# Linear attention with routed experts: deeper load buffers, later expert weights, and scatters that skip empty slots and do not order each other

## The chip, the cores and the metric

The kernel runs on one core of a Trainium2 chip. The metric is the device time of one execution in microseconds; the time before is the median of five runs. A core has five engines that run their own queues in order: TensorE (PE in the profile, with PEld for its weight loads), VectorE (DVE), ScalarE (ACT), GpSimd (POOL) and SyncE (SP). DMAs are issued from GpSimd's and SyncE's queues and run on 16 DMA engines.

## The reference

`q`, `k`, `v` are [8, 8, 576, 64] (batch, heads, sequence, head width). Softmax of q is over the head width, softmax of k over the sequence; the attention output has its heads put side by side, so that it is a table of 4608 tokens by 512. Every token belongs to one of eight experts, by `domain_id`, and goes through that expert's two matrices with a ReLU between them.

```
q_s = exp(q - max(q)); q_s = q_s / sum(q_s, over d)
k_s = exp(k - max(k)); k_s = k_s / sum(k_s, over s)
kv  = einsum('bhsd,bhse->bhde', k_s, v)
x   = einsum('bhsd,bhde->bhse', q_s, kv)      # then to [4608, 512]
for e in range(8):
    m = domain_id == e
    out[m] = relu(x[m] @ w1[e]) @ w2[e]       # w1 512x1024, w2 1024x512
```

Inputs and output are float32. The kernel works in float16 with float32 sums.

## The kernel before

It has two parts, and the instructions are put in order by a scheduler that follows what depends on what and how many buffers a pool has; the text of the program gives the priority.

**Attention, per batch (`emit_batch`).** Three DMAs of GpSimd's queue load k, q and v of the batch (96 partitions, each six sequence rows of eight heads) and turn them to float16. `k_raw` and `q_raw` share one tag of the pool `apool`, which has two buffers, so there is one buffer for each; `v_sb` has two. ScalarE makes `ke` and `qe` (exponentials, L323 and L326). VectorE adds the six rows of `ke` in five instructions (L335 to L339, tiles `ks01`, `ks23`, `ks45`). TensorE transposes `qe` in 24 pieces (L346), which ScalarE copies from PSUM to `qT_sb` in three instructions (L353). For each of four pairs of heads TensorE computes k transposed times v (L360, 12 matmuls into `kv_ps`) and the column sums of `ke`, by one matmul of `ks01` with a column of ones (L367, into `tab_ps`); VectorE takes the reciprocal and scales the pair into the block matrix `kvp` (L375 to L382). For each of six rows j, TensorE multiplies `qT_sb` by `kvp` into two tiles, `xpsA` and `xpsB` (L397; the tag has two buffers), and VectorE divides each by its softmax sum into `x_sb` (L408, L410). A DMA of SyncE's queue writes `x_sb` to `attn_x_scratch` (L416).

**Routing.** Each expert has 704 slots, 5632 in all, for 4608 tokens. Early instructions on VectorE give each token its slot and a second slot behind the expert's count, so that most empty slots get a copy of a token. The table from slot to token is made with compares (`emit_mask_chunk`, four chunks, tiles `spm` and `sce`, L254 to L274) and matmuls, and ends in `perms_sb` (L305).

**Experts, per group of 512 slots (11 groups, `emit_gather` and `emit_group`).** Four indirect DMAs of GpSimd's queue gather 128 token rows each (L449); TensorE transposes them (L470), multiplies by w1 (L493), ScalarE applies ReLU (L501), TensorE multiplies by w2 (L512), VectorE copies each 128 rows to `out_stage` (L519), and an indirect DMA of GpSimd's queue scatters them to the output rows (L531). Slots of a second copy write the same values to the same row once more. Since all scatters write the one output tensor, each waits until the scatter before it has landed. `xG` has three buffers.

**Weights.** `load_weights(e)` (L144) issues two DMAs of 1024 KB (as float16) on GpSimd's queue; `wpool` has four buffers. In the text, experts 0 and 1 stand behind the last batch, and expert 2 and later ones in the loop over groups, by this table:

```
late_load = {0: [2], 1: [3], 2: [4], 3: [5], 5: [6], 6: [7]}
```

Loads of experts 0 to 3 wait for no buffer, and the scheduler puts them wherever GpSimd's queue has nothing of higher priority.

## Time and profile before

| | us |
|---|---|
| median of five runs | 378.2 |
| lowest and highest | 377.34, 379.39 |
| the profiled execution | 379.95 |
| its span, first to last instruction | 378.2 |

| engine | busy us | share of the span |
|---|---|---|
| TensorE, matmuls | 257.4 | 68% |
| TensorE, weight loads | 159.1 | 42% |
| VectorE | 151.6 | 40% |
| GpSimd | 120.5 | 32% |
| ScalarE | 113.0 | 30% |

The mean granted clock of TensorE is 0.821 of its full 2.4 GHz. The shares are means over stages that differ: the attention stage ends with the first gather, at 153 us, the expert stage's matmuls run from 164 to 348 us, and behind them the core still writes. So each stage is to be read by itself: which engine is busy in it, and which wait ends last.

### The profile page before, as it was taken

The numbers are of one execution on the slowest core, as the hardware profiler recorded it, in microseconds if no ns is written. First come the engines' busy times: TensorE is split into PE (matmuls) and PEld (weight loads), VectorE is DVE, ScalarE is ACT, GpSimd is POOL, SyncE is SP. The second block draws the span as 40 slices with busy tenths as digits, with TensorE's granted clock in tenths as the row PEclk, the third lists the DMA queues.
The fourth block names the chain that finished last, engine by engine and source line by source line (L and its number), as shares of the span: only waits on it lengthen the run. The fifth ranks groups of instructions, "written<-read, shape, count | busy, mean of one in ns | idle before, by whom it ended". The sixth has DMA issues, their size and how long they took to land.

```text
span 378.2 us, 4999 instructions
## 1 busy us (share of the span) xinstructions
PE 257.4 (68%) x2010; PEld 159.1 (42%) x2010; DVE 151.6 (40%) x488; ACT 113.0 (30%) x129; POOL 120.5 (32%) x143
## 2 busy tenths in 40 slices
PE   0365547545484874279999999999998897988000
PEld 0353426424363552134756445575544455533000
DVE  7986566687374896022240322403223021222000
ACT  2573746270706300022404225042240222231000
POOL 5320302122110000673726244360644353223232
PEclk9999999655555555569999999999999698999655
DMA  6999999999999314232399676269269222122111
GB/s 95 204 209 204 184 216 230 204 236 206 240 205 237 54 51 125 72 99 81 113 180 206 125 135 163 71 149 197 88 125 231 90 98 97 57 83 83 58 75 64
DMA packets 38055, 53.32 MB, mean 141 GB/s; under 512 B 2320, under 2 KB 28944, under 8 KB 38032
## 3 DMA queue, kind: packets, MB, share of 16 engines
q0 software_dynamic: 36992, 48.24, 64.5%
q1 hardware_dynamic: 1040, 4.76, 3.6%
q8 instruction: 16, 0.26, 0.3%
q14 instruction: 7, 0.06, 0.0%
HBM read 67.67 MB, written 16.25 MB: 222 GB/s over the span
## 4 chain that ended last, share of the span: by engine, by line
PE 39%; DMA 33%; issue 17%; ACT 4%; DVE 3%; POOL 3%; POOLq 0%; ACTq 0%; DVEq 0%
PE hT_ps L493 20%; PE out_ps L512 18%; DMA q_raw<-in_q_dram 15%; DMA out_dram<-out_stage,perms_sb 9%; DMA k_raw<-in_k_dram 7%; DMA xG<-attn_x_scratch,perms_sb 2%; POOL xG L449 2%; ACT qe L326 2%; DVE xT L478 1%; ACT ke L323 1%; DVE out_stage L519 1%; ACT qT_sb L353 1%; PE tpsA L470 1%; POOLq L592 0%; POOL out_dram L531 0%
## 5 line engine op out<-in xcount | busy, mean ns | idle before, releaser
L501 ACT ACTIVATE hT_sb<-hT_ps 128x512 f16<-128x512 f32 x88 | 50.6, 596 | 158.2 <-PE hT_ps L493 158.0
L493 PE MATMUL hT_ps<-xT,w_sb 128*128 128x512 f16 (+7 forms) x576 | 84.6, 309 | 4.0 <-DVE xT L478 4.0
L519 DVE COPY out_stage<-out_ps 128x512 f32<-128x512 f32 x44 | 30.4, 692 | 140.2 <-PE out_ps L512 140.2
L512 PE MATMUL out_ps<-w_sb,hT_sb 128*128 128x512 f16 (+1 forms) x384 | 82.0, 380 | 0.0
L531 POOL DMA_INDIRECT out_dram<-out_stage,perms_sb x44 | 43.4, 986 | 115.3 <-DMA out_dram<-out_stage,perms_sb 57.7
L493 PEld LDWEIGHTS <-w_sb 128*128 128x128 f16 x576 | 50.5, 102 | 35.9 <-issue 6.3
L449 POOL DMA_INDIRECT xG<-attn_x_scratch,perms_sb x44 | 42.3, 961 | 50.6 <-issue 50.2
L512 PEld LDWEIGHTS <-hT_sb 128*128 128x128 f16 (+1 forms) x384 | 36.2, 100 | 42.8 <-issue 2.9
L397 PEld LDWEIGHTS <-qT_sb 128*96 128x96 f16 x192 | 23.9, 174 | 37.7 <-DVE x_sb L410 29.3
L346 PE MATMUL qT_ps<-ident,qe 96*128 96x96 f16 x192 | 19.5, 279 | 23.0 <-ACT qe L326 12.3
L397 PE MATMUL xpsA<-kvp,qT_sb 128*96 128x130 f16 x96 | 22.2, 318 | 18.5 <-DVE x_sb L410 11.7
L326 ACT ACTIVATE qe<-q_raw 96x3072 f16<-96x3072 f16 x8 | 22.1, 2764 | 29.4 <-DMA q_raw<-in_q_dram 29.3
L323 ACT ACTIVATE ke<-k_raw 96x3072 f16<-96x3072 f16 x8 | 22.1, 2766 | 23.1 <-DMA k_raw<-in_k_dram 15.2
L397 PE MATMUL xpsB<-kvp,qT_sb 128*96 128x130 f16 x96 | 22.6, 321 | 8.3 <-DVE x_sb L410 5.7
L360 PE MATMUL kv_ps<-v_sb,ke 96*64 96x64 f16 x384 | 19.9, 241 | 10.5 <-DMA v_sb<-in_v_dram 8.5
L346 PEld LDWEIGHTS <-qe 96*128 96x128 f16 x192 | 16.2, 140 | 23.8 <-ACT qe L326 22.9
L360 PEld LDWEIGHTS <-ke 96*64 96x64 f16 x384 | 16.8, 149 | 17.5 <-issue 8.7
L353 ACT COPY qT_sb<-qT_ps 128x768 f16<-128x768 f16 x24 | 17.5, 801 | 17.2 <-PE qT_ps L346 10.8
L470 PEld LDWEIGHTS <-xG 128*128 128x128 f16 x176 | 12.0, 105 | 23.1 <-DMA xG<-attn_x_scratch,perms_sb 10.6
L470 PE MATMUL tpsA<-ident,xG 128*128 128x128 f16 x88 | 9.5, 246 | 17.4 <-DMA xG<-attn_x_scratch,perms_sb 15.5
L410 DVE TENSOR_TENSOR x_sb<-xpsB,rq 96x256 f16<-96x256 f32 x48 | 20.0, 417 | 0.5
L410 DVE TENSOR_TENSOR x_sb<-xpsA,rq 96x256 f16<-96x256 f32 x48 | 20.0, 417 | 0.5
(86 smaller groups left out, 170.1 us busy)
## 6 DMA issues: line engine op xcount, KB each, us to landing
w_sb<-in_moe_w_dram POOLq DMA_DIRECT2D x16, 1024.0 KB, 14.2
k_raw<-in_k_dram POOLq DMA_DIRECT2D x8, 576.0 KB, 11.4
q_raw<-in_q_dram POOLq DMA_DIRECT2D x8, 576.0 KB, 11.7
v_sb<-in_v_dram POOLq DMA_DIRECT2D x8, 576.0 KB, 11.1
attn_x_scratch<-x_sb SPq DMA_DIRECT2D x8, 576.0 KB, 5.9
xG<-attn_x_scratch,perms_sb POOLq DMA_INDIRECT x44, 2.8
out_dram<-out_stage,perms_sb POOLq DMA_INDIRECT x44, 2.7
dom<-in_moe_domain_id_dram SPq DMA_DIRECT2D x1, 36.0 KB, 1.8
```

The costliest lines, as they stand in the source:

```text
L323: nc.scalar.activation(out=ke[0:SPB].rearrange("p j (h d) -> p h j d", d=D), in_=k_sb[0:SPB], func=AF.Exp)
L326: nc.scalar.activation(out=qe[0:SPB].rearrange("p j (h d) -> p h j d", d=D), in_=q_sb[0:SPB], func=AF.Exp)
L346: nc.tensor.transpose(out=tE[idx % 3][:, idx // 3, 0:SPB], in_=qe[0:SPB, j, 128 * hp : 128 * hp + 128], identity=ident[0:SPB, 0:SPB],)
L360: nc.tensor.matmul(out=kn[64 * hh : 64 * hh + 64, 0, 0:D], lhsT=ke[0:SPB, j, 64 * h : 64 * h + 64], rhs=v_sb[0:SPB, h, j, :], start=(j == ...
L397: nc.tensor.matmul(out=t[0:SPB, hp // 2, 0:130], lhsT=qT_sb[:, j * HP + hp, :], rhs=kv[:, hp, :], start=True, stop=True,)
L410: nc.vector.tensor_tensor(out=xout, in0=blk[:, :, :, 0:64], in1=rq[0:SPB].unsqueeze(3).to_broadcast([SPB, 2, 2, D]), op=ALU.mult,)
L449: nc.gpsimd.indirect_dma_start(out=xG[:, jj, :], out_offset=None, in_=x_dram, in_offset=bass.IndirectOffsetOnAxis(ap=perms_sb[:, 4 * g + j ...
L493: nc.tensor.matmul(out=hT_pair[i][:, c0:c1], lhsT=w1_sb[:, kc, fb * P : (fb + 1) * P], rhs=xT[:, kc, c0:c1], start=(kc == 0), stop=(kc == ...
L501: nc.scalar.activation(out=hT_sb[:, 2 * fbp + i, :], in_=hT_pair[i][:, :], func=AF.Relu)
L512: nc.tensor.matmul(out=out_ps[lo:hi, :], lhsT=hT_sb[:, fb, P * jj + lo : P * jj + hi], rhs=w2_sb[:, fb, :], start=(fb == 0), stop=(fb == F ...
L519: nc.vector.tensor_copy(out=out_stage[:, jj, :], in_=out_ps[:, :])
L531: nc.gpsimd.indirect_dma_start(out=out, out_offset=bass.IndirectOffsetOnAxis(ap=perms_sb[:, 4 * g + jj : 4 * g + jj + 1], axis=0), in_=out ...
```

## The change

- A new pool `lpool` with three buffers for each of `k_raw`, `q_raw` and `v_sb`, in place of two for k and q together and two for v.
- The weight DMAs of experts 2 and 3 get an order behind the gathers that stand before them in the text (12 gathers for expert 2, 16 for expert 3).
- The five adds of `ke` go. The column sums are taken by six matmuls, one for each row j, that add up in PSUM.
- From batch 2 on, the exponential of q stands on ScalarE behind the `qT_sb` copies of the batch two before.
- A second table, `scat_sb`: for slots at or beyond an expert's count, 8192 is added to the row number. Seven VectorE instructions on 352 columns, five small ones and one iota make it. The scatters use it with a bounds check, which skips the rows beyond 4607. The gathers keep `perms_sb`.
- Each scatter is declared independent of all scatters before it.

The diff, cut to its core:

```
+    lpool = sb_stack.enter_context(tc.tile_pool(name="lpool", bufs=3))
     def load_weights(e):
+        if e in (2, 3):
+            for d in (d1, d2):
+                tc.add_manual_dep(
+                    d.ins, first_gathers[-1],
...
+    cnt_sb = cpool.tile([P, E], FP32, name="cnt_sb")
+    nc.vector.tensor_copy(out=cnt_sb[:, :], in_=tot_ps[:, 0, 0:E])
     def emit_perms():
+        nc.vector.tensor_tensor(out=thr[:, :, :], in0=thr[:, :, :], in1=em0[:, :, :], op=ALU.mult)
+        thr2 = cpool.tile([P, NSC], FP32, name="thr2")
+        nc.vector.tensor_reduce(out=thr2[:, :], in_=thr[:, :, :], op=ALU.add, axis=AXX)
+        w2f = cpool.tile([P, NSC], FP32, name="w2f")
+        nc.vector.tensor_tensor(out=w2f[:, :], in0=s_f[:, :], in1=thr2[:, :], op=ALU.is_ge)
...
+        nc.vector.tensor_tensor(out=scat_sb[:, :], in0=perms_sb[:, :], in1=w2i[:, :], op=ALU.add)
     def emit_batch(b):
-        k_sb = apool.tile([P, H, J, D], FP16, tag="raw", name="k_raw")
-        q_sb = apool.tile([P, H, J, D], FP16, tag="raw", name="q_raw")
-        v_sb = apool.tile([P, H, J, D], FP16, tag="v_sb", name="v_sb")
+        k_sb = lpool.tile([P, H, J, D], FP16, tag="kr", name="k_raw")
+        q_sb = lpool.tile([P, H, J, D], FP16, tag="qr", name="q_raw")
+        v_sb = lpool.tile([P, H, J, D], FP16, tag="v_sb", name="v_sb")
+        if b >= 2:
+            tc.add_manual_dep(
+                q_exp.ins, qT_last[b - 2],
...
-        nc.vector.tensor_tensor(out=ks01[0:SPB], in0=ke[0:SPB, 0], in1=ke[0:SPB, 1], op=ALU.add)
...
-            nc.tensor.matmul(
-                out=tab_ps[:, 400 + hp : 401 + hp],
-                lhsT=ks01[0:SPB, 128 * hp : 128 * hp + 128],
...
+            for j in range(J):
+                nc.tensor.matmul(
+                    out=tab_ps[:, 400 + hp : 401 + hp],
+                    lhsT=ke[0:SPB, j, 128 * hp : 128 * hp + 128],
...
     def emit_group(g):
-                nc.gpsimd.indirect_dma_start(
+                scat = nc.gpsimd.indirect_dma_start(
                     out=out,
-                        ap=perms_sb[:, 4 * g + jj : 4 * g + jj + 1], axis=0
+                        ap=scat_sb[:, 4 * g + jj : 4 * g + jj + 1], axis=0
...
+                    bounds_check=N - 1,
+                    oob_is_err=False,
+                for old in scatters:
+                    tc.declare_no_dep(scat.ins, old, reason="disjoint rows")
```

The edit moves instructions. GpSimd's queue at the end of the attention loads, before. In brackets is what an instruction waits for: DMASW0 to DMASW7 are eight completion counters that the DMAs of this queue use, an engine's name is work of that engine. The numbers in `w1_sb_2` and the like are the experts.

```order
L150 DMA w2_sb_2_1896<-in_moe_w2_dram 128x8x512 [waits DMASW1_49]
L147 DMA w1_sb_3_2021<-in_moe_w1_dram 128x4x1024 [waits DMASW2_49]
L320 DMA v_sb_1467<-in_v_dram 96x8x384 [waits PE_49]
L318 DMA k_raw_1660<-in_k_dram 96x8x384 [waits DMASW0_49,Activation_49]
L319 DMA q_raw_1661<-in_q_dram 96x8x384 [waits DMASW7_49,DMASW5_49,Activation_49]
L150 DMA w2_sb_3_2022<-in_moe_w2_dram 128x8x512 [waits DMASW6_49]
L320 DMA v_sb_1662<-in_v_dram 96x8x384 [waits PE_49]
L449 DMA xG_1880<-attn_x_scratch,perms_sb_188 128x512 [waits DMAHW1_49,DMAHW0_49,DMAHW2_49,DMASW7_49,DMAHW3_49,DMASW5_49,DMAHW4_49,DMASW4_49,DMAHW5_49,DMASW3_49,DMAHW6_49,DVE_49,DMAHW7_49,PE_49,Activation_49]
```

And now:

```order
L370 DMA k_raw_1770<-in_k_dram 96x8x384 [waits DMASW5_49,Activation_49]
L371 DMA q_raw_1771<-in_q_dram 96x8x384 [waits DMASW6_49,Activation_49]
L149 DMA w1_sb_0_1977<-in_moe_w1_dram 128x4x1024 [waits DMASW7_49]
L152 DMA w2_sb_0_1978<-in_moe_w2_dram 128x8x512 [waits DMASW0_49]
L372 DMA v_sb_1772<-in_v_dram 96x8x384 [waits DMASW1_49,PE_49]
L149 DMA w1_sb_1_1981<-in_moe_w1_dram 128x4x1024 [waits DMASW2_49]
L152 DMA w2_sb_1_1982<-in_moe_w2_dram 128x8x512 [waits DMASW3_49]
L501 DMA xG_2003<-attn_x_scratch,perms_sb_193 128x512 [waits DMAHW2_49,DMAHW3_49,DMAHW1_49,DMAHW4_49,DMAHW0_49,DMAHW5_49,DMASW4_49,DMAHW6_49,DVE_49,DMAHW7_49,PE_49,Activation_49]
```

Before, the weights of expert 3 (and, farther up, those of experts 0 to 2) stand among the loads of q, k and v. Now only those of expert 0 stand ahead of the last v, those of expert 1 behind it, and the gathers follow; experts 2 and 3 come after them.

GpSimd's queue where the first scatters stand, before:

```order
L531 DMA out_0_dram<-out_stage_1971,perms_sb_188 4608x512 [waits DMASW0_49,DVE_49]
L531 DMA out_0_dram<-out_stage_1971,perms_sb_188 4608x512 [waits DMASW1_49,DMASW0_49,DVE_49]
L449 DMA xG_2182<-attn_x_scratch,perms_sb_188 128x512 [waits DMASW2_49,PE_49]
L531 DMA out_0_dram<-out_stage_1971,perms_sb_188 4608x512 [waits DMASW3_49,DMASW1_49,DVE_49]
L449 DMA xG_2182<-attn_x_scratch,perms_sb_188 128x512 [waits DMASW4_49]
L449 DMA xG_2182<-attn_x_scratch,perms_sb_188 128x512 [waits DMASW5_49]
L449 DMA xG_2182<-attn_x_scratch,perms_sb_188 128x512 [waits DMASW6_49]
L531 DMA out_0_dram<-out_stage_1971,perms_sb_188 4608x512 [waits DMASW7_49,DMASW3_49,DVE_49]
L147 DMA w1_sb_4_2187<-in_moe_w1_dram 128x4x1024 [waits PE_49]
```

And now:

```order
L149 DMA w1_sb_3_2152<-in_moe_w1_dram 128x4x1024 [waits DMASW6_49]
L584 DMA out_0_dram<-out_stage_2094,scat_sb_194 4608x512 [waits DMASW7_49,DVE_49]
L152 DMA w2_sb_3_2153<-in_moe_w2_dram 128x8x512 [waits DMASW0_49]
L584 DMA out_0_dram<-out_stage_2094,scat_sb_194 4608x512 [waits DMASW1_49,DVE_49]
L584 DMA out_0_dram<-out_stage_2094,scat_sb_194 4608x512 [waits DMASW2_49,DVE_49]
L584 DMA out_0_dram<-out_stage_2094,scat_sb_194 4608x512 [waits DMASW3_49,DVE_49]
L501 DMA xG_2321<-attn_x_scratch,perms_sb_193 128x512 [waits DMASW4_49,PE_49]
```

Before, a scatter waits for up to two DMA counters, one of them that of the scatter before it. Now it waits for one, used eight DMAs earlier, and for VectorE's copy; the gathers of a group stand together behind the four scatters, and the weights of expert 3 among them.

ScalarE's queue around the copies of batch 4 (`qT_sb_1045` before, `qT_sb_1091` now), before:

```order
L353 COPY qT_sb_843<-qT_ps2_846 128x8x96 [waits PE_49]
L323 ACTIVATE ke_1033<-k_raw_1027 96x8x6x64 [waits DMASW7_49,DVE_49,Activation_49]
L326 ACTIVATE qe_1034<-q_raw_1028 96x8x6x64 [waits DMASW0_49,Activation_49]
L323 ACTIVATE ke_1271<-k_raw_1265 96x8x6x64 [waits DVE_49,DMASW3_49,PE_49,Activation_49]
L353 COPY qT_sb_1045<-qT_ps0_1046 128x8x96 [waits PE_49]
L353 COPY qT_sb_1045<-qT_ps1_1047 128x8x96
L353 COPY qT_sb_1045<-qT_ps2_1048 128x8x96
L326 ACTIVATE qe_1272<-q_raw_1266 96x8x6x64 [waits DMASW4_49,Activation_49]
L326 ACTIVATE qe_1472<-q_raw_1466 96x8x6x64 [waits DMASW0_49,Activation_49]
```

And now:

```order
L402 COPY qT_sb_877<-qT_ps1_879 128x8x96
L402 COPY qT_sb_877<-qT_ps2_880 128x8x96
L378 ACTIVATE qe_1088<-q_raw_1082 96x8x6x64 [waits DMASW5_49,Activation_49]
L378 ACTIVATE qe_1338<-q_raw_1332 96x8x6x64 [waits DMASW0_49,Activation_49]
L375 ACTIVATE ke_1337<-k_raw_1331 96x8x6x64 [waits DMASW7_49,PE_49]
L402 COPY qT_sb_1091<-qT_ps0_1092 128x8x96 [waits PE_49]
L402 COPY qT_sb_1091<-qT_ps1_1093 128x8x96
L402 COPY qT_sb_1091<-qT_ps2_1094 128x8x96
L378 ACTIVATE qe_1570<-q_raw_1564 96x8x6x64 [waits DMASW3_49,Activation_49]
```

Before, batch 4's copies stand behind the exponential of batch 5's k alone. Now they stand behind the exponentials of both its q and its k, each of which waits for its load.

## Rows read from the trace of the kernel before

**Rows 1.** the page's 40 equal slices of the span: busy tenths

```profile
PE   0365547545484874279999999999998897988000
...
DMA  6999999999999314232399676269269222122111
```

**Rows 2.** transfers and weight issues, 0 to 125 us: count, KB, us to landing

```profile
DMA packets 25756, 25.62 MB, mean 205 GB/s; under 512 B 731, under 2 KB 23219, under 8 KB 25747
...
w_sb<-in_moe_w_dram POOLq DMA_DIRECT2D x8, 1024.0 KB, 16.1
```

**Rows 3.** the chain that ended last: start us, us, what

```profile
115.93 36.15 issue
...
346.96 0.66 issue
```

**Rows 4.** timeline, 142 to 166 us: start us, us, engine, what, idle before

```profile
148.42 0.30 SPq L416 DMA_DIRECT2D attn_x_scratch<-x_sb  x1
153.37 1.04 POOL L449 DMA_INDIRECT xG<-attn_x_scratch,perms_sb  x1 [37.44 <-issue]
```

**Rows 5.** timeline of TensorE in the expert stage, with the first and last group

```profile
164.47 8.74 PE L493 MATMUL hT_ps<-xT,w_sb 128*128 128x512 f16 x32
...
276.62 7.08 PE L493 MATMUL hT_ps<-xT,w_sb 128*128 128x512 f16 x32 [0.45 <-DVE xT L478]
...
293.97 0.23 PE L470 MATMUL tpsA<-ident,xG 128*128 128x128 f16 x1 [2.25 <-DMA xG<-attn_x_scratch,perms_sb]
...
333.96 7.08 PE L493 MATMUL hT_ps<-xT,w_sb 128*128 128x512 f16 x32 [1.61 <-DVE xT L478]
340.87 7.07 PE L512 MATMUL out_ps<-w_sb,hT_sb 128*128 128x512 f16 x32
```

**Rows 6.** timeline of GpSimd's queue: a gather and the last scatter

```profile
157.27 0.95 POOL L449 DMA_INDIRECT xG<-attn_x_scratch,perms_sb  x1 [0.30 <-issue]
...
373.72 0.97 POOL L531 DMA_INDIRECT out_dram<-out_stage,perms_sb  x1 [2.52 <-DMA out_dram<-out_stage,perms_sb]
```

**Rows 7.** the page's costliest groups: the scatters, busy and mean, idle before them

```profile
L531 POOL DMA_INDIRECT out_dram<-out_stage,perms_sb x44 | 43.4, 986 | 115.3 <-DMA out_dram<-out_stage,perms_sb 57.7
```

**Rows 8.** timeline at the end: the last copy to the staging tile

```profile
347.98 0.69 DVE L519 COPY out_stage<-out_ps 128x512 f32<-128x512 f32 x1 [1.03 <-PE out_ps L512]
```

**Rows 9.** stretches: busy us of PE, PEld, DVE, ACT, POOL; clock, DMA, GB/s

```profile
0.00:153.00 153.00, 79.97 (x874) 60.96 (x874) 106.41 (x400) 62.43 (x41) 27.63 (x47) 0.73 1.01 179
...
130.00:140.00 10.00, 8.05 (x83) 5.45 (x80) 9.30 (x45) 2.20 (x3) 0.00 (x0) 0.50 0.20 59
```

**Rows 10.** groups by line and shape: busy us, mean ns, idle before

```profile
L254 DVE TENSOR_TENSOR spm<-lo7h,i128h 128x2304 f16<-128x2304 f16 x4 | 10.2, 2545 | 0.0
...
L367 PE MATMUL tab_ps<-ones,ks 96*128 96x1 f16 x32 | 6.4, 200 | 0.7 <-DVE rk L375 0.6
...
L261 DVE TENSOR_TENSOR sce<-hi7h,i44h 128x792 f16<-128x792 f16 x4 | 3.9, 969 | 0.0
L335 DVE TENSOR_TENSOR ks<-ke 96x512 f16<-96x512 f16 x8 | 3.3, 407 | 6.9 <-ACT ke L323 6.8
```

**Rows 11.** timeline of the first 24 us

```profile
8.09 0.45 DVE L191 TENSOR_TENSOR slotsel<-slotsel,onehot 128x288 f32<-128x288 f32 x1
...
16.23 1.89 PEld L346 LDWEIGHTS <-qe 96*128 96x128 f16 x24
...
23.32 0.27 PE L397 MATMUL xpsA<-kvp,qT_sb 128*96 128x130 f16 x1 [0.67 <-DVE kvp L382]
```

**Rows 12.** timeline of VectorE: where the x tiles of three batches begin

```profile
121.23 0.18 DVE L408 RECIPROCAL rq<-xpsA 96x4 f32<-96x4 f32 x1 [4.88 <-PE xpsA L397]
...
132.61 0.18 DVE L408 RECIPROCAL rq<-xpsA 96x4 f32<-96x4 f32 x1
...
141.33 0.18 DVE L408 RECIPROCAL rq<-xpsA 96x4 f32<-96x4 f32 x1
```

More of the change, by code (lines that the diff above doesn't have):

```diff
@@ L142 @@
     wt = {}
+    first_gathers = []
     def load_weights(e):
@@ L153, in load_weights @@
         wt[e] = (w1_sb, w2_sb)
+        if e in (2, 3):
+            for d in (d1, d2):
+                tc.add_manual_dep(
+                    d.ins, first_gathers[-1],
+                    mybir.DependencyInfo(mybir.DependencyClass.NoSync, mybir.DependencyReason.DATA),
+                    reason="behind the first gathers",
+                )
     ps_stack = ExitStack()
@@ L312, in emit_perms @@
         )
+        s_i = cpool.tile([P, NSC], I32, name="s_i")
+        nc.gpsimd.iota(s_i[:, :], pattern=[[P, NSC]], base=0, channel_multiplier=1)
+        s_f = cpool.tile([P, NSC], FP32, name="s_f")
+        nc.vector.tensor_copy(out=s_f[:, :], in_=s_i[:, :])
+        em0 = cpool.tile([P, NSC, E], FP32, name="em0")
+        nc.vector.tensor_tensor(
+            out=em0[:, :, :],
+            in0=s_f[:, :].unsqueeze(2).to_broadcast([P, NSC, E]),
+            in1=ecap_f[:, :].unsqueeze(1).to_broadcast([P, NSC, E]),
+            op=ALU.is_ge,
+        )
@@ new lines, in emit_perms @@
+        em1 = cpool.tile([P, NSC, E], FP32, name="em1")
+        nc.vector.tensor_scalar(
+            out=em1[:, :, :], in0=ecap_f[:, :].unsqueeze(1).to_broadcast([P, NSC, E]),
+            scalar1=float(CAP), scalar2=None, op0=ALU.add,
+        )
+        nc.vector.tensor_tensor(
+            out=em1[:, :, :],
+            in0=s_f[:, :].unsqueeze(2).to_broadcast([P, NSC, E]),
+            in1=em1[:, :, :],
+            op=ALU.is_lt,
+        )
+        nc.vector.tensor_tensor(out=em0[:, :, :], in0=em0[:, :, :], in1=em1[:, :, :], op=ALU.mult)
@@ new lines, in emit_perms @@
+        thr = cpool.tile([P, NSC, E], FP32, name="thr")
+        nc.vector.tensor_tensor(
+            out=thr[:, :, :],
+            in0=cnt_sb[:, :].unsqueeze(1).to_broadcast([P, NSC, E]),
+            in1=ecap_f[:, :].unsqueeze(1).to_broadcast([P, NSC, E]),
+            op=ALU.add,
+        )
+        nc.vector.tensor_tensor(out=thr[:, :, :], in0=thr[:, :, :], in1=em0[:, :, :], op=ALU.mult)
+        thr2 = cpool.tile([P, NSC], FP32, name="thr2")
+        nc.vector.tensor_reduce(out=thr2[:, :], in_=thr[:, :, :], op=ALU.add, axis=AXX)
@@ L325, in emit_batch @@
         )
-        nc.scalar.activation(
+        q_exp = nc.scalar.activation(
             out=qe[0:SPB].rearrange("p j (h d) -> p h j d", d=D), in_=q_sb[0:SPB], func=AF.Exp
         )
-        kv = kvp[b % 2]
-        ks01 = apool.tile([P, H * D], FP16, tag="ks01", name="ks01")
-        ks23 = apool.tile([P, H * D], FP16, tag="ks23", name="ks23")
-        ks45 = apool.tile([P, H * D], FP16, tag="ks45", name="ks45")
-        nc.vector.tensor_tensor(out=ks01[0:SPB], in0=ke[0:SPB, 0], in1=ke[0:SPB, 1], op=ALU.add)
-        nc.vector.tensor_tensor(out=ks23[0:SPB], in0=ke[0:SPB, 2], in1=ke[0:SPB, 3], op=ALU.add)
-        nc.vector.tensor_tensor(out=ks45[0:SPB], in0=ke[0:SPB, 4], in1=ke[0:SPB, 5], op=ALU.add)
-        nc.vector.tensor_tensor(out=ks01[0:SPB], in0=ks01[0:SPB], in1=ks23[0:SPB], op=ALU.add)
-        nc.vector.tensor_tensor(out=ks01[0:SPB], in0=ks01[0:SPB], in1=ks45[0:SPB], op=ALU.add)
+        if b >= 2:
+            tc.add_manual_dep(
+                q_exp.ins, qT_last[b - 2],
+                mybir.DependencyInfo(mybir.DependencyClass.NoSync, mybir.DependencyReason.DATA),
+                reason="copies of batch b-2 first",
+            )
+        kv = kvp[b % 2]
         qT_sb = apool.tile([P, J * HP, SPB], FP16, tag="qT_sb", name="qT_sb")
@@ L352, in emit_batch @@
         for r in range(3):
-            nc.scalar.copy(out=qT_sb[:, r : J * HP : 3, :], in_=tE[r][:, :, 0:SPB])
+            qT_copy = nc.scalar.copy(out=qT_sb[:, r : J * HP : 3, :], in_=tE[r][:, :, 0:SPB])
+        qT_last[b] = qT_copy.ins.name
         for hp in range(HP):
@@ L434 @@
     xg_tiles = {}
+    scatters = []
     def emit_gather(g):
@@ L537, in emit_group @@
                     in_offset=None,
-                )
+                    bounds_check=N - 1,
+                    oob_is_err=False,
+                )
+                for old in scatters:
+                    tc.declare_no_dep(scat.ins, old, reason="disjoint rows")
+                scatters.append(scat.ins)
     for b in range(B):
```

19 lines of the change are left out of this document (12 added, 7 removed).

## The prediction

> **What bounds the kernel now.** I read the 40-slice table first, then the chain of waits, then the timeline around each place where the chain changes its kind. The slices [rows 1] show three stretches. In the first thirteen slices the DMA row is at 9. In the middle TensorE is at 9. In the last three TensorE is at 0 and the core still moves data.
>
> Stage one (attention) is fed by transfers. Over 0 to 125 us 25.6 MB move at 205 GB/s, and eight of the expert weight loads (1024 KB each) are among them [rows 2], that is experts 0 to 3. The chain runs through a transfer of q and then through a long piece whose only end is the first gather [rows 3]: the last loads are in at about 123 us (thirteen slices of 9.46), the last batch is worked off, its result is written at 148.42 us, and the first gather starts at 153.37 us [rows 4].
>
> Stage two (experts) is one of TensorE, but only for a while. The eight 512-row groups start their first matmuls from 164.47 to 276.62 us, that is every 16.02 us; then come holes [rows 5]. They come from GpSimd's queue: a gather takes 1.25 us of it (0.95 and 0.30 of idling before), a scatter 3.49 (0.97 and 2.52), since each scatter waits for the one before to land [rows 6]; the group of all 44 scatters idles 115.3 us, half of it for a scatter's own DMA [rows 7]. Per group of rows that is 4 x 3.49 + 4 x 1.25 = 19.0 us, plus weight loads, against TensorE's 16.0: the queue falls behind, and gathers stand behind late scatters.
>
> Stage three is what is left of that backlog: TensorE's last matmuls end at 347.9 us (340.87 + 7.07) [rows 5], the last copy to the staging tile starts at 347.98 [rows 8], and seven more scatters follow, 3.5 us apart, the last issued at 373.72 [rows 6].
>
> **The change, part by part.**
>
> *Scatters without mutual waits.* In the new order a scatter waits for its copy and for the DMA issued eight places earlier. Then it costs what a gather costs, 1.25 us of queue [rows 6]. I have no row of a scatter that checks its bounds. Below: 0.97 us busy, as now, and at best a little less data, since 1024 of the 5632 slots are empty and are skipped. Above: twice that, a guess as wide as I can make it from the rows, since no DMA of this queue shows a longer issue than about 1 us. I take 1.25 us with the gap, the gather being the nearest row. Then the queue needs 8 x 1.25 = 10.0 us per group plus weights, under 16.0, and never falls behind.
>
> Tail: the last scatter follows its copy: 347.98 + 0.69 of copy + 0.66 as the chain shows between copy and scatter [rows 3, 8] = 349.3 instead of 373.7. Gain 24.4 us. At twice the price the last group's four scatters follow copies that come 1.72 us apart (1.03 and 0.69) about 3 us later: gain 21.
>
> Holes in stage two: at the pace of the first eight groups the last group's first matmuls begin at 276.62 + 3 x 16.02 = 324.7 instead of 333.96, and TensorE ends after 7.08 + 7.07 us, at 338.8 instead of 347.9 [rows 5]. Gain 9.1 us; a lower bound are the two waits shown, 2.25 for a gather and 1.61, together 3.9 us.
>
> *Weights of experts 2 and 3 behind the first gathers, three buffers for k, q and v.* Four weight loads of 1.05 MB, 4.2 MB at 205 GB/s = 20.5 us, leave the transfer-bound stage. In the new order the weights of experts 0 and 1 also stand behind nearly all loads. So the last v is in after 24 loads (14.2 MB) and two weight loads (2.1 MB): 79.4 us, from about 6 us on, plus about 1 us for each of seven writes that share the engines: 92 us instead of 123. Weights of expert 1 land 10 us later, still before the gathers. Experts 2 and 3 are issued 15 and 22 us after the first gather and take two times 10 us; they are used some 44 and 75 us after it. That costs nothing; if the slack were gone, 10 us.
>
> *What is then late.* VectorE. It is busy 106.4 us of the 153 before the gathers [rows 9]. The change removes 40 adds (five lines of 3.2 us like the one shown = 16.1 us) [rows 10] and adds twelve small instructions: seven on 352 columns near 0.45 us, by the row on 288 columns [rows 11], and five I put at 0.2, together 4 us. Left: 94 us, so the write of the last batch cannot leave before about 96 us. That is the lower end.
>
> The likely value comes from the pace. A period on VectorE is one batch's x tiles woven with the next batch's kv pieces. With all loads there it took 132.61 to 141.33 = 8.7 us; the one before took 121.23 to 132.61 = 11.4 us, with the transposes of a later batch and five adds (1.7 us) in it, so 9.7 without them; the last batch alone took 141.33 to 148.42 = 7.1 us [rows 12, 4]. Batch 0's kv is ready near 23 us, when its x matmuls start [rows 11]. From there: six periods of 9.7, one of 8.7, then 7.1 = 97. To this come the mask chunks left over then (four chunks of 5.8 us: 10.2 for the large compares, three lines of 3.9 like the one shown, 1.4 for a copy [rows 10]; less 10 that fit under the first loads, so 13.2), 4 us of new instructions and 0.7 of table work: 115. I add 3 us for two waits: ScalarE now places batch 4's copies behind the exponentials of batch 5, which need a load that lands near 58 us by the count above, and TensorE makes six small matmuls for each sum where it made one.
>
> *The sums on TensorE.* 32 matmuls of 0.20 us [rows 10] become 192. Twenty-four loads of 128 columns took 1.89 us, 0.079 us each [rows 11], so six take 0.47: 0.27 more, 32 times, 8.6 us on an engine that is busy 80.0 us of 153 [rows 9]. It hides under VectorE's 9.7 us period unless it delays the x matmuls; at worst 4 x 0.27 per period, 7.6 us in seven.
>
> By the Trainium skill (TensorE: Matmul & The Clock Gate, section LDWEIGHTS) a weight load takes its columns divided by 1.2 ns, 107 ns here; the row of this trace shows 79. By the page the six would take 0.64 us, TensorE would get 14 us more instead of 8.6, and the worst case of the sentence above would be 12 us. The measurement decides, and the rest stands without this.
>
> So the last write leaves at 118 us instead of 148.4: gain 30.4. Late end: all seven periods at 11.4 plus 1.1 for the sums, and 5 us for loads: 23 + 87.5 + 7.1 + 18 + 5 = 140, gain 8. Early end: the 96 us above, gain 52, though no stretch is without gaps; rival (b) gives the nearest I believe. What follows (write, gathers, transposes: 148.42 to 164.47 [rows 4, 5]) keeps its 16.05 us.
>
> **The sum.** 30.4 + 9.1 + 24.4 = 63.9 us. The profiled execution has a span of 378.2 us and took 379.95, so 316 on its own scale; it is 1.75 us above the median of the five runs, so 314 against that.
>
> **The rivals.**
> (a) *The pace of stage one does not improve so much.* TensorE, VectorE and ScalarE work in the given order, each tile of x waiting for the other's buffer, and the sums stand in between. For it: 11.4 us in the one period that had transposes. Against it: 9.7 once the adds are gone. With 11.4 plus 1.1 in all seven the last write is at about 135: gain 13, time 331.
> (b) *Stage one is quicker.* VectorE is 93% busy from 130 to 140 us, where no load is missing [rows 9]; 94 us of work at that share is 101 us, and with the first 6 us before work begins 107: gain 41, time 304.
> (c) *The bounds check makes a scatter dear.* At 2 us with its gap doubled the queue needs 4 x 2.3 + 5.0 + 1.8 = 16 us per group, just TensorE's pace: 8 us lost, time 322.
> (d) *Slower than before.* The same mechanism, farther: the queue would bind all of stage two. From a first gather at 123 us the queue has 7 us of idling, 44 gathers (55 us), twelve weight loads (11 us) and 44 scatters to do by 374, so a scatter would have to occupy it 4.0 us, four times its row. That is where the sign turns; at 5 us the kernel takes about 420. Nothing in the trace speaks for it.
> (e) *The scatters still wait* (the declaration without effect). Then only stage one gains, and the backlog of 19 us per group returns: 378 - 30 = 348. The new order lists only one DMA wait on each scatter, the one eight places back, so this is nearly excluded.
>
> **How the numbers follow.** Forecast (309 to 320) 0.56; (a) 0.18; (b) 0.12; (c) 0.09; (d) 0.02; (e) 0.03. The likeliest is 314 us. From 302 to 330 all but (d), (e), the late half of (a) and the earliest part of (b) are held, about 8 in 10. About 0.3% is what a measurement of this kernel can tell from no change. Faster 0.97, same 0.01, slower 0.02: only (d) lies on the other side.
>
> **What would show it.** The first thirteen slices should become about ten; the last v lands near 92 us; the last write of x at 110 to 126 us; VectorE above 85% busy between 30 and 110 us. Groups start every 15 to 16.3 us up to the last, with no wait for a gather. After TensorE's last matmul less than 8 us follow, and scatters stand 1.25 us apart or as far as their copies. I am wrong in stage one if VectorE idles for TensorE in every period, and in stage two if a scatter's busy time is far from 1 us or TensorE waits for w of expert 2.

## The result, and the profile after

The changed kernel takes 315.8 us (median of 8 runs, 315.11 to 316.45) against 378.2 us (median of 15): a ratio of 0.835, 95% interval 0.833 to 0.836. The forecast was 314. The profiled execution took 315.93 us with a span of 314.2.

The borders of the three stages, read from the same rows as before ([rows 4 to 6, 8]), in us:

| | before | after | gain, measured | gain, forecast |
|---|---|---|---|---|
| last write of x | 148.42 | 118.13 | 30.3 | 30.4 |
| first matmul of the first group | 164.47 | 133.97 | 30.5 | 30.4 |
| first matmul of the last group | 333.96 | 294.79 | 39.2, that is 8.7 more | 9.1 more |
| last scatter issued | 373.72 | 309.78 | 63.9, that is 24.8 more | 24.4 more |

The page's 40 slices (7.86 us each now) answer to [rows 1]:

```profile
PE   0168896858888870399999999999999999989793
...
PEclk9999998555655555579999999999999999999998
DMA  5999999999999323359999999579994322020102
```

TensorE's row is at 9 from slice 17 to slice 34 (counted from 0) without the holes of before, and it ends in the last slice and not three slices ahead of it. The DMA row is at 9 up to slice 12, 102 us, where I had expected some ten slices of before, 95 us: the weights of expert 1 still land there. The clock row stands at half (1.2 of 2.4 GHz) from slice 7 to slice 16 and at full from slice 18 on; TensorE was busy 0.6 to 0.9 of the slices before it fell, and without a break from 134 us on before it rose.

The timelines, start, duration, engine and what, then the idle time ahead and what ended it. TensorE's first and last groups, SyncE's last write, VectorE's last copy and GpSimd's last two scatters:

```profile
118.13 0.30 SPq L467 DMA_DIRECT2D attn_x_scratch<-x_sb  x1
...
133.97 9.10 PE L546 MATMUL hT_ps<-xT,w_sb 128*128 128x512 f16 x32
...
294.79 7.08 PE L546 MATMUL hT_ps<-xT,w_sb 128*128 128x512 f16 x32 [1.61 <-DVE xT L531]
301.71 7.07 PE L565 MATMUL out_ps<-w_sb,hT_sb 128*128 128x512 f16 x32
...
308.06 0.98 POOL L584 DMA_INDIRECT out_dram<-out_stage,scat_sb  x1 [0.74 <-DVE out_stage L572]
308.81 0.69 DVE L572 COPY out_stage<-out_ps 128x512 f32<-128x512 f32 x1 [1.03 <-PE out_ps L565]
309.78 0.98 POOL L584 DMA_INDIRECT out_dram<-out_stage,scat_sb  x1 [0.74 <-DVE out_stage L572]
```

A scatter now follows its copy by 0.28 us and the scatter ahead by 1.72, the pace of the copies; what ends its wait is VectorE, not a DMA. The group of all 44, to be held against [rows 7] (busy us, mean ns, idle before and its main cause):

```profile
L584 POOL DMA_INDIRECT out_dram<-out_stage,scat_sb x44 | 44.0, 1000 | 67.0 <-DVE out_stage L572 48.1
```

A scatter that checks its bounds costs 1000 ns, against 986. Idling ahead of the scatters fell from 115.3 us to 67.0, of which 48.1 are waits for VectorE's copies.

### The profile page after: what moved, and what is told of

Same layout as the page of the kernel before. It is cut to its first block, busy times and chain, and to the rows that moved or that the text cites. A ratio compares the mean times of both kernels' runs of the same rounds, so it can differ in the third digit from the quotient of the medians.

```text
span 314.2 us, 5338 instructions
## 1 busy us (share of the span) xinstructions
PE 255.0 (81%) x2170; PEld 162.5 (52%) x2170; DVE 142.4 (45%) x460; ACT 112.3 (36%) x129; POOL 121.5 (39%) x144
## 4 chain that ended last, share of the span: by engine, by line
PE 42%; issue 17%; DMA 15%; DVE 12%; POOL 9%; ACT 3%; POOLq 1%; DVEq 0%; ACTq 0%
PE out_ps L565 16%; PE hT_ps L546 16%; DMA q_raw<-in_q_dram 8%; DMA v_sb<-in_v_dram 6%; POOL out_dram L584 5%; DVE x_sb L461 5%; POOL xG L501 3%; PE kv_ps L410 3%; PE qT_ps L395 2%; DVE rq L459 2%; DVE xT L531 1%; PE xpsA L448 1%; PE xpsB L448 1%; DVE out_stage L572 1%; DMA attn_x_scratch<-x_sb 1%
## 5 line engine op out<-in xcount | busy, mean ns | idle before, releaser
L554 ACT ACTIVATE hT_sb<-hT_ps 128x512 f16<-128x512 f32 x88 | 50.6, 596 | 150.0 <-PE hT_ps L546 149.8
L572 DVE COPY out_stage<-out_ps 128x512 f32<-128x512 f32 x44 | 30.4, 692 | 131.5 <-PE out_ps L565 131.5
L546 PE MATMUL hT_ps<-xT,w_sb 128*128 128x512 f16 (+7 forms) x576 | 81.1, 301 | 4.1 <-DVE xT L531 4.0
L584 POOL DMA_INDIRECT out_dram<-out_stage,scat_sb x44 | 44.0, 1000 | 67.0 <-DVE out_stage L572 48.1
L501 POOL DMA_INDIRECT xG<-attn_x_scratch,perms_sb x44 | 42.5, 966 | 62.1 <-issue 56.7
L546 PEld LDWEIGHTS <-w_sb 128*128 128x128 f16 x576 | 48.8, 99 | 34.2 <-issue 4.6
L448 PEld LDWEIGHTS <-qT_sb 128*96 128x96 f16 x192 | 23.3, 174 | 22.2 <-DVE x_sb L461 17.3
L448 PE MATMUL xpsA<-kvp,qT_sb 128*96 128x130 f16 x96 | 21.4, 318 | 7.5 <-DVE x_sb L461 4.2
L448 PE MATMUL xpsB<-kvp,qT_sb 128*96 128x130 f16 x96 | 21.7, 320 | 5.1 <-DVE x_sb L461 4.0
L410 PE MATMUL kv_ps<-v_sb,ke 96*64 96x64 f16 x384 | 21.1, 239 | 5.5 <-DMA v_sb<-in_v_dram 4.3
L395 PE MATMUL qT_ps<-ident,qe 96*128 96x96 f16 x192 | 19.6, 278 | 6.0 <-ACT qT_sb L402 3.8
L372 POOL DMA_DIRECT2D v_sb<-in_v_dram x8 | 6.3, 783 | 41.4 <-PE kv_ps L410 24.2
L523 PEld LDWEIGHTS <-xG 128*128 128x128 f16 x176 | 11.6, 103 | 18.0 <-issue 9.7
L395 PEld LDWEIGHTS <-qe 96*128 96x128 f16 x192 | 16.4, 140 | 6.5 <-issue 4.0
## 6 DMA issues: line engine op xcount, KB each, us to landing
k_raw<-in_k_dram POOLq DMA_DIRECT2D x8, 576.0 KB, 17.3
```

What stands on the lines that cost most here:

```text
L395: nc.tensor.transpose(out=tE[idx % 3][:, idx // 3, 0:SPB], in_=qe[0:SPB, j, 128 * hp : 128 * hp + 128], identity=ident[0:SPB, 0:SPB],)
L410: nc.tensor.matmul(out=kn[64 * hh : 64 * hh + 64, 0, 0:D], lhsT=ke[0:SPB, j, 64 * h : 64 * h + 64], rhs=v_sb[0:SPB, h, j, :], start=(j == ...
L448: nc.tensor.matmul(out=t[0:SPB, hp // 2, 0:130], lhsT=qT_sb[:, j * HP + hp, :], rhs=kv[:, hp, :], start=True, stop=True,)
L501: gat = nc.gpsimd.indirect_dma_start(out=xG[:, jj, :], out_offset=None, in_=x_dram, in_offset=bass.IndirectOffsetOnAxis(ap=perms_sb[:, 4 * ...
L546: nc.tensor.matmul(out=hT_pair[i][:, c0:c1], lhsT=w1_sb[:, kc, fb * P : (fb + 1) * P], rhs=xT[:, kc, c0:c1], start=(kc == 0), stop=(kc == ...
L554: nc.scalar.activation(out=hT_sb[:, 2 * fbp + i, :], in_=hT_pair[i][:, :], func=AF.Relu)
```

## The experiments

Every experiment was timed beside the kernel before, on the same chip. Beside all of them but one, on three chips, that kernel took 386 us and not 378; beside one more, on the last of these chips, it took 379. So times are given as ratios to it, or as differences to a run of the changed kernel beside the same 386 us (327.15 us, the first run below), and stages are read from the traces. "The first trace" of either kernel is that of the section above, "the second" the one taken here.

### The changed kernel again, and the kernel before again

No edit.

> The changed kernel once more, beside the three edits of it that follow, so that they are compared on the same chip: 0.835 of the kernel before. On the chip of the runs before this one the kernel before takes 386 us instead of 378; if what is slower there lies in the scatter backlog, the changed kernel stays at 316 us, and if it is a slower chip throughout, it takes 322 us.

It took 327.15 us, 0.847 of the kernel before (0.845 to 0.849). The traced execution took 324.97 us, with a span of 323.2, 9.0 longer than in the first trace. The first stage is the same (last write at 117.9 us), and so are the last three groups (303.80 - 255.49 = 48.3 us, as 294.79 - 246.48). From the first group to the last it took 303.80 - 133.73 = 170.1 us instead of 160.8, and that is the whole difference of the two traces.

```profile
133.73 9.21 PE L546 MATMUL hT_ps<-xT,w_sb 128*128 128x512 f16 x32
...
303.80 7.08 PE L546 MATMUL hT_ps<-xT,w_sb 128*128 128x512 f16 x32 [1.61 <-DVE xT L531]
```

In these stretches TensorE and ScalarE wait for each other, here in the fifth group:

```profile
204.02 1.91 PE L546 MATMUL hT_ps<-xT,w_sb 128*128 128x64 f16 x16 [0.48 <-issue]
...
206.24 0.60 ACT L554 ACTIVATE hT_sb<-hT_ps 128x512 f16<-128x512 f32 x1 [1.58 <-PE hT_ps L546]
206.89 1.91 PE L546 MATMUL hT_ps<-xT,w_sb 128*128 128x64 f16 x16 [0.96 <-issue]
207.67 0.60 ACT L554 ACTIVATE hT_sb<-hT_ps 128x512 f16<-128x512 f32 x1 [0.83 <-issue]
```

In the first trace the same group runs its 52 matmuls in one piece of 6.95 us. ScalarE's waits ahead of its ReLUs, over all groups, in the trace of this run (us in total, times, longest; the 34.1 us lie ahead of the first group):

```profile
ACT hT_sb L554 <- PE hT_ps L546: 109.1, 50, 10.5
ACT hT_sb L554 <- DMA xG<-attn_x_scratch,perms_sb: 34.1, 1, 34.1
ACT hT_sb L554 <- issue: 11.0, 8, 8.6
ACT hT_sb L554 <- remote: 4.8, 4, 2.3
```

In the first trace they all go to TensorE's matmuls (149.8 us in 63 waits). "Remote" and "issue" are waits whose end the profile doesn't show.

> The kernel before once more, for its trace on the chip of the other experiments, where it takes 386 us and not 378, and the changed kernel 327 and not 316. Theory A (the chip is slower wherever ScalarE and TensorE hand tiles to each other in the expert stage, as in the changed kernel's trace there, 9 us between the first and the last group): stage one ends as before at 148 us, and the eight groups that came every 16.0 us come every 17. Theory B (transfers are slower there): stage one ends later than 150 us.

This one run took 378.6 us, beside 379.05, so neither theory could be looked at. But it says that the chip alone isn't the cause: shortly before, the same chip gave 386. What made the difference stays open. Its last write of x stands at 149.5 us, 1.1 later than in the first trace of the kernel before; so far can two traces of one kernel lie apart.

### Scatters in order again

```
-                for old in scatters:
-                    tc.declare_no_dep(scat.ins, old, reason="disjoint rows")
```

> The changed kernel without the declaration that scatters are independent; the table and the bounds check stay. My theory: stage one keeps its gain (last x write at 118 us), but each scatter again waits for the one before to land, 3.5 us of GpSimd's queue each, 19 us per group against TensorE's 16, and seven scatters are left after the last matmul: 378 - 30 = 348 us. Rival (skipped rows make a scatter short, so that the bounds check alone takes the backlog away): under 330 us, scatters less than 2 us apart. A rival by which the holes come from elsewhere: 316 us as the changed kernel.

0.927 of the kernel before (0.922 to 0.932; the forecast of 348 in 378.2 is 0.920), 358.45 us, 31 us more than the changed kernel (327.15). The first stage kept its gain (last write at 118.0). The scatters, first the group of 44, then the last two:

```profile
L584 POOL DMA_INDIRECT out_dram<-out_stage,scat_sb x44 | 44.0, 1000 | 121.3 <-DMA out_dram<-out_stage,scat_sb 59.1 <-DVE out_stage L572 27.5 <-issue 26.4
```

```profile
349.87 0.98 POOL L584 DMA_INDIRECT out_dram<-out_stage,scat_sb  x1 [2.52 <-DMA out_dram<-out_stage,scat_sb]
353.31 0.98 POOL L584 DMA_INDIRECT out_dram<-out_stage,scat_sb  x1 [2.46 <-DMA out_dram<-out_stage,scat_sb]
```

The table and the bounds check are in, and still the 2.5 us of waiting are back, and with them holes and tail. TensorE's transposes wait for gathers (us in total, times, longest; first this run, then the changed kernel):

```profile
PE tpsA L523 <- DMA xG<-attn_x_scratch,perms_sb: 26.2, 11, 8.4
```

```profile
PE tpsA L523 <- DMA xG<-attn_x_scratch,perms_sb: 10.7, 3, 8.4
```

Two intervals between the starts of neighbouring groups are 23.4 and 25.9 us long; the longest of the changed kernel is 17.3 in its first trace and 18.3 in its second. From the last group's first matmul to the last scatter it takes 37.7 us (315.64 to 353.31) instead of 15.0.

```profile
315.64 7.08 PE L546 MATMUL hT_ps<-xT,w_sb 128*128 128x512 f16 x32 [1.61 <-DVE xT L531]
```

The rival by which skipped rows shorten a scatter falls.

### Independent scatters alone

The kernel before, with the code that makes `scat_sb`, and this:

```
-                nc.gpsimd.indirect_dma_start(
+                scat = nc.gpsimd.indirect_dma_start(
-                        ap=perms_sb[:, 4 * g + jj : 4 * g + jj + 1], axis=0
+                        ap=scat_sb[:, 4 * g + jj : 4 * g + jj + 1], axis=0
+                    bounds_check=N - 1,
+                    oob_is_err=False,
+                for old in scatters:
+                    tc.declare_no_dep(scat.ins, old, reason="disjoint rows")
```

The second table must come along: without it two scatters may write one row in any order, and independent scatters by `perms_sb` weren't tried.

> The kernel before with only the second table, the bounds check and the independent scatters. My theory: stage one as before plus at most 4 us of VectorE work for the table (last write 148 to 152 us), holes gone (9.1) and tail gone (24.4): 378.2 - 33.5 = 344.7 us, 345 to 349. Rival (the holes are made by the gathers standing behind weight loads, not by the scatters): only the tail goes, 354 us.

0.941 (0.935 to 0.948): 21.6 us less, where I expected 33.5. The time is nearer to the rival's 354 of 378.2 (0.936) than to mine, so the traces must tell the two apart. The tail went as expected: 15.0 us from the last group's first matmul to the last scatter, against 39.8 before.

```profile
344.03 7.08 PE L536 MATMUL hT_ps<-xT,w_sb 128*128 128x512 f16 x32 [1.61 <-DVE xT L521]
```

```profile
357.29 0.98 POOL L574 DMA_INDIRECT out_dram<-out_stage,scat_sb  x1 [0.74 <-DVE out_stage L562]
359.02 0.98 POOL L574 DMA_INDIRECT out_dram<-out_stage,scat_sb  x1 [0.74 <-DVE out_stage L562]
```

The waits for gathers went too: 10.9 us, those of the start, are left of 15.5. The last two intervals between groups, in which the kernel before has its holes, take 34.2 us instead of 42.5. But the groups as a whole did not come faster: 344.03 - 166.57 = 177.5 us from the first to the last, against 169.5 before, with 22.9 us for the first interval alone. TensorE's waits in this stretch name the unexplained hand-overs again, 13 us of them:

```profile
PE hT_ps L536 <- issue: 6.9, 5, 2.8
PE hT_ps L536 <- ACT hT_sb L544: 6.2, 6, 1.7
```

The last write stands at 150.5 us, 2.1 later than in the first trace of the kernel before and 1.0 later than in the second; that bounds what the table costs. So 24.8 us of the tail are shown. That the holes come from ordered scatters is shown by their coming back in the run before this one and going in this one; that they are worth 8.7 us of the whole time is shown only by the two first traces, since here waits of another kind took their place.

### Late weights alone, deep loads alone

Two kernels, each the kernel before with one edit.

```
+        if e in (2, 3):
+            for d in (d1, d2):
+                tc.add_manual_dep(d.ins, first_gathers[-1], ...)
```

```
+    lpool = sb_stack.enter_context(tc.tile_pool(name="lpool", bufs=3))
-        k_sb = apool.tile([P, H, J, D], FP16, tag="raw", name="k_raw")
+        k_sb = lpool.tile([P, H, J, D], FP16, tag="kr", name="k_raw")
```

and the same for q and v.

> The kernel before with only the weights of experts 2 and 3 behind the first gathers. Theory A (stage one is bound by bytes, so every MB counts): 4.2 MB at 205 GB/s less, last write 128 us, and the scatter backlog as before, 358 us. Theory B (one buffer for k and one for q hold the loads back, and weights only fill the holes between them): last write later than 138 us, the DMA engines idle instead, 368 to 378 us.

> The kernel before with only three buffers for each of k, q and v; in its order five of the eight weight loads of experts 0 to 3 stand ahead of the last v and three behind, without any rule for the weights. Theory A (bytes): all 22.6 MB still pass before the last batch is done, last write about 140 to 148 us, 370 to 378 us. Theory B (depth lets k, q and v go ahead of the weights): the last v lands near 107 us and VectorE, which still has its 16 us of adds, ends near 134 us: 364 us.

Late weights: 0.998 (0.995 to 1.002), last write at 143.9 us. Deep loads: 0.947 (0.942 to 0.953), 20 us less, last write at 131.1. So theory B held both times, for deep loads with a time 6 us better than its 364 (0.947 of 378.2 is 358). SyncE's writes of x, first of late weights, then of deep loads (start of the first and time to the end of the last, in the window up to 152 us):

```profile
113.42 30.81 SPq L424 DMA_DIRECT2D attn_x_scratch<-x_sb  x4
```

```profile
114.00 17.42 SPq L417 DMA_DIRECT2D attn_x_scratch<-x_sb  x3
```

To take 4.2 MB out of the first stage is worth only 4.5 us of it while k and q have one buffer each: the DMA engines idle instead (from 90 to 100 us they move 103 GB/s, where the kernel before moves 231). And it is lost again in the second stage, which takes 182.3 us from the first group to the last (159.93 to 342.22), against 169.5 before, with 25.9 us of waits for gathers. To give k, q and v three buffers is worth 17.3 us with no rule for the weights: the scheduler then issues three of the eight weight loads behind the last v by itself. In the deep loads' second stage TensorE waits only 10.9 us for gathers although the scatters are ordered; the groups there take 177.6 us, again with late hand-overs, and the queue's lateness shows in the tail alone (37.1 us).

### The changed kernel without the rule for the weights

```
-        if e in (2, 3):
+        if e in ():
```

> The changed kernel without the rule that puts the weights of experts 2 and 3 behind the first gathers; in its order the four loads then stand right behind those of expert 1, still behind the last v. Theory A (three buffers alone put k, q and v ahead of the weights): last write of x at 117 to 119 us as with the rule, and the 20 us of transfers pass before the gathers, within 1% of the changed kernel. Theory B (the bytes share the engines with the last loads and with the writes of x): last write 4 to 20 us later.

0.865 (0.863 to 0.868), 334.42 us. Last write at 117.9 us, theory A; but the first gather starts at 124.94 us and TensorE's first group at 136.11, instead of 133.73 in the second trace of the changed kernel. So 2.4 us lie between the last write and the first group: 18.2 us here, 15.9 with the rule. The rest lies in the second stage (177.7 us from the first group to the last, against 170.1), most of it in the first interval between groups: 23.1 us against 17.2. There ScalarE waits for hand-overs that I can't explain:

```profile
144.64 0.60 ACT L554 ACTIVATE hT_sb<-hT_ps 128x512 f16<-128x512 f32 x1 [2.25 <-PE hT_ps L546]
147.48 1.57 ACT L554 ACTIVATE hT_sb<-hT_ps 128x512 f16<-128x512 f32 x3 [2.24 <-PE hT_ps L546]
```

The two other runs without the rule beside the same 386 us, independent scatters alone and deep loads alone, have the same long first interval, 22.9 and 23.8 us; with the rule it is 16.4 to 17.7 in every run. Beside the 378 us it is 16.8 without the rule and 17.1 with it. So the rule is worth 7.3 us here, 2.4 of them ahead of the first group and the rest by waits whose cause is open, and the time lies beyond the 1% I gave.

### Adds back, one sum, copies first

```
+        nc.vector.tensor_tensor(out=ks01[0:SPB], in0=ke[0:SPB, 0], in1=ke[0:SPB, 1], op=ALU.add)
...
-            for j in range(J):
                 nc.tensor.matmul(
                     out=tab_ps[:, 400 + hp : 401 + hp],
-                    lhsT=ke[0:SPB, j, 128 * hp : 128 * hp + 128],
+                    lhsT=ks01[0:SPB, 128 * hp : 128 * hp + 128],
```

> The changed kernel with the five adds on VectorE back and one matmul for each column sum. Theory A (VectorE binds stage one): 16.1 us more on an engine that is busy 81% there, so the last write comes 12 to 16 us later, 328 to 332 us. Theory B (TensorE at half clock binds it): 8.6 us less on TensorE, the last write up to 8 us earlier, 308 to 316 us. Both in turn: within 5 us of the changed kernel.

336.78 us, 9.6 more than the changed kernel (327.15). Last write at 129.1 us, 11.2 later, for 16.1 us of adds: theory A in kind, at 0.7 of the price and just short of its 12 to 16 us.

```profile
109.38 20.01 SPq L475 DMA_DIRECT2D attn_x_scratch<-x_sb  x3
```

With the runs above this gives the first stage in steps: 148.4 us before, 131.1 with deep loads alone, 129.1 with all of the change except that the adds stay, 117.9 with all of it. So of 30.5 us the buffers give 17.3, the adds 11.2, and all else together 2.0.

```
-            for j in range(J):
-                    lhsT=ke[0:SPB, j, 128 * hp : 128 * hp + 128],
+                    lhsT=ke[0:SPB, 0, 128 * hp : 128 * hp + 128],
```

> The changed kernel with one matmul of row 0 alone for each column sum: five sixths of the sum are left out, so it is a price only. 160 small matmuls less, no add more. Theory A (VectorE binds, the sums are hidden): within 1 us. Theory B (the six matmuls stand in TensorE's order between pieces that VectorE waits for): 32 x 0.27 = 8.6 us at most, of which I expect 3 to 5, at half clock up to 12.

326.85 us, 0.3 less; last write at 117.4, 0.5 earlier. The six matmuls are hidden: theory A.

```
+        if b == 5:
+            for x_exp in (q_exp, k_exp):
+                tc.add_manual_dep(x_exp.ins, qT_last[b - 1], ...)
```

> The changed kernel with the exponentials of batch 5 on ScalarE behind the copies of batch 4 instead of ahead of them. In the trace the three copies waited from 56.1 us (transposes done) to 64.6, and VectorE's period there took 17.7 us instead of 11.6. Theory A (this wait is on the path): last write 4 to 6 us earlier, 310 to 312 us. Theory B (the loads of that time set the pace, batch 5's own k and q come late anyway): within 1.5 us.

325.12 us, 2.0 less, with runs (322.63 to 327.24) that overlap those of the changed kernel (324.97 to 328.12); last write at 116.9, 1.0 earlier: theory B. The rows that I had taken for a loss of 6 us, ScalarE in the changed kernel:

```profile
59.27 2.76 ACT L378 ACTIVATE qe<-q_raw 96x3072 f16<-96x3072 f16 x1 [5.58 <-DMA q_raw<-in_q_dram]
...
61.94 2.75 ACT L375 ACTIVATE ke<-k_raw 96x3072 f16<-96x3072 f16 x1
...
64.59 2.17 ACT L402 COPY qT_sb<-qT_ps 128x768 f16<-128x768 f16 x3
```

The copies stand behind two exponentials, of which the first waits 5.58 us for its load. With the copies first, VectorE's period there fell from 17.7 to 15.0 us, but the next rose from 12.5 to 14.1: more than half of it was lost again there. The other order that the change sets, the exponential of q behind the copies of the batch two before, was never run by itself.

### The scalings on ScalarE

```
-            nc.vector.tensor_tensor(
-                out=kv[0:64, hp, 0:64],
-                in0=kn[0:64, 0, 0:64],
-                in1=rk[0:64, 0:1].to_broadcast([64, 64]),
-                op=ALU.mult,
+            nc.scalar.activation(
+                out=kv[0:64, hp, 0:64], in_=kn[0:64, 0, 0:64], func=AF.Copy, scale=rk[0:64, 0:1],
             )
```

and the same for the lower half.

> The changed kernel with the 64 scalings of kv_ps into kvp on ScalarE (activation with the reciprocal as scale) instead of VectorE: 32 x (0.18 + 0.23) = 13.1 us off VectorE, some 64 x 0.25 us on ScalarE. Theory A (VectorE binds stage one; 16.1 us of adds moved the last write by 11.2 us, 0.7 of their price): last write 7 to 10 us earlier. Theory B (ScalarE's order, in which a scaling stands behind exponentials that wait for loads, takes it back): last write no more than 2 us earlier, or later.

0.832 (0.828 to 0.835), 321.25 us against 327.15: 1.8% faster than the changed kernel. The kernel before took 386.4 us beside both. Last write 112.8 us, 5.1 earlier than in the second trace of the changed kernel; a scaling takes 0.31 us on ScalarE, not 0.25. That lies between the two theories: 13.1 us off VectorE give 0.4 of their price. That ScalarE's order takes the rest back is likely (it is busy 61.6 of the 80 us from 30 to 110, where it had 44.8), but no run shows it.

```profile
112.83 0.30 SPq L461 DMA_DIRECT2D attn_x_scratch<-x_sb  x1
```

> The kernel of the run before it, with batch 4's copies ahead of batch 5's exponentials on ScalarE, and without the copy inside each mask chunk (4 x 0.35 us of VectorE). Theory A: each adds a little, last write 1 to 3 us earlier than with the scalings moved alone. Theory B (loads or ScalarE bind once VectorE has been relieved): within 1 us.

0.836 (0.833 to 0.839), 323.14 us, last write at 114.2, 1.4 later than with the scalings alone: not faster, and just outside the 1 us of theory B. Which of the two additions costs it was not tried.

## Why the prediction held, step by step

**The scatters.** The step was: each waits for the one before to land, 2.5 us; take that away and a scatter costs what a gather does. With ordered scatters the waits, the holes and the tail are back; with independent scatters alone the tail and the late holes go. The measured gains are 24.8 us for the tail (forecast 24.4; a scatter follows its copy by 0.28 us, where I had put 0.66) and 8.7 us for the holes (9.1). The unknown price of the bounds check, for which I had kept a rival, is 14 ns. Groups came every 16.1 us in the mean (294.79 - 133.97 over ten), but single intervals run from 14.8 to 17.3, and four of the ten lie outside the band of 15 to 16.3 that I gave. The first (17.1) is long because TensorE's first matmuls still run at half clock, as the clock of 0.50 shows (9.10 us for 32 of them instead of 7.08):

```profile
134.00:138.00 4.00, 4.00 (x12) 1.48 (x11) 0.76 (x2) 0.97 (x2) 3.18 (x4) 0.50 0.35 98
```

**The first stage.** 30.3 us against 30.4, and the seven periods of VectorE sum to 87.5 us where I had counted 87.8. So the size of the whole was right, but three of its parts were not, and an agreement to 0.1 us is in part luck.

- *What brings the loads forward.* I reckoned by bytes: four weight loads leave, 20.5 us. The experiments give the depth of the buffers the credit: 17.3 us by itself, the rule for the weights 4.5 by itself, and beside the depth nothing up to the last write and 2.4 up to the first group. The last v landed when forecast (issued at 74.37 us, 17.8 to 20.0 us under way, so 92 to 94; forecast 92). But its issue had waited for a buffer, not for other transfers: GpSimd's queue idled 10.64 us until TensorE had read the old v.

```profile
74.37 0.78 POOL L372 DMA_DIRECT2D v_sb<-in_v_dram  x1 [10.64 <-PE kv_ps L410]
```

  The trace of before could have told it: there the queue idled 23.6 us ahead of loads of k until ScalarE had read the old k, and 19.6 us ahead of loads of q in the same way.

```profile
L318 POOL DMA_DIRECT2D k_raw<-in_k_dram x8 | 6.4, 806 | 41.3 <-ACT ke L323 23.6 <-DMA q_raw<-in_q_dram 17.6
L319 POOL DMA_DIRECT2D q_raw<-in_q_dram x8 | 6.2, 779 | 21.2 <-ACT qe L326 19.6 <-ACT ke L323 1.6
```

- *VectorE.* It is on the path, as forecast: the adds cost 0.7 of their price, the scalings 0.4. But it does not bind alone: it was busy 64.7 of the 80 us from 30 to 110, 81%, and not above 85%. These are the rows of the windows (busy us of PE, PEld, DVE, ACT, POOL; clock, DMA share, GB/s):

```profile
30.00:110.00 80.00, 64.47 (x830) 53.22 (x829) 64.72 (x258) 44.83 (x33) 11.11 (x15) 0.66 1.16 213
```

  The periods are far from even: 14.7, 10.6, 17.7, 12.5, 11.5, 11.6 and 8.8 us, with mask chunks in the first, third and fourth, and the late load of q in the third. And the sign by which I would be wrong in stage one showed: in each of the seven periods VectorE waits for TensorE, between 0.3 and 4.8 us, 15.5 us in all.

```profile
DVE rq L459 <- PE xpsA L448: 7.7, 12, 2.8
DVE rq L459 <- PE xpsB L448: 5.1, 13, 1.4
DVE rk L426 <- PE tab_ps L418: 2.7, 4, 1.8
```

  My count of 87.8 us holds 74.7 us of work (8.1 in each period, by the two of before below less 1.7 for the adds of the first, and 17.9 for chunks, new instructions and table) and so 13.1 us of idling. The seven periods hold 70.0 of work and 17.6 of idling: two misses that cancel, and that is the luck. The windows, the two of before first:

```profile
121.23:132.61 11.38, 9.48 (x104) 7.03 (x105) 9.81 (x44) 5.03 (x5) 0.00 (x0) 0.50 0.46 81
132.61:141.33 8.72, 7.06 (x64) 4.67 (x64) 8.10 (x37) 0.24 (x1) 0.00 (x0) 0.50 0.16 48
```

```profile
23.43:110.96 87.53, 70.52 (x911) 58.30 (x910) 69.96 (x278) 49.09 (x34) 12.03 (x16) 0.69 1.16 210
```

  The 3 us that I had put in for two waits was a lump; moving the copies gives 1.0 us back, the sums 0.5.
- *The sums on TensorE.* I had 8.6 us more, by a weight load of 79 ns. Measured: 10.6 us for 192 matmuls, against 6.4 for 32 [rows 10], so 4.2 more. The matmuls (busy us, mean ns), the single loads (shortest, median, longest ns), and loads in a row:

```profile
L418 PE MATMUL tab_ps<-ones,ke 96*128 96x1 f16 x192 | 10.6, 170 | 4.7 <-ACT ke L375 4.7
...
L418 PEld LDWEIGHTS <-ke x192: 95/104/152, 11.7 to 107.5; 96*128 96x128 f16 x192
...
25.02 0.24 PEld L418 LDWEIGHTS <-ke 96*128 96x128 f16 x6
...
31.70 0.36 PEld L418 LDWEIGHTS <-ke 96*128 96x128 f16 x6
...
105.12 0.36 PEld L418 LDWEIGHTS <-ke 96*128 96x128 f16 x6
```

  One load takes 104 ns in the median, and six in a row take 0.24 to 0.36 us, since they overlap. So the 79 ns that I had read [rows 11] was the distance from load to load in a row of 24, not the time of one; neither figure may be multiplied by six. The sums hid under VectorE all the same. The Trainium skill (TensorE: Matmul & The Clock Gate, section LDWEIGHTS), by which the columns divided by 1.2 are the ns of a load, gives 107 ns for one; the median of 104 agrees.

**From the last write to the first group** nothing changed: 15.84 us against 16.05 [rows 4, 5]. That cover held because the rule kept 4.2 MB away from it: without the rule it grew to 18.2 us.

**The scale.** The whole miss of 1.8 us is the last step of the sum. The profiled execution of before had come out 1.75 us above its median, and I took that off the forecast; the profiled execution of after lies 0.13 above its own. On the scale of profiled executions the forecast was 316 and the result 315.93.

**The rivals.** The slower pace in all periods (331) fell to the last write at 118 us instead of 135, the quicker first stage (304) to VectorE's 81% instead of 93%, and the dear bounds check (322) and scatters of 4 us or more (420 at 5) to the mean of 1000 ns. Scatters that still wait (348) fell to what ends their waits, VectorE's copies and not a DMA.
